# Sketched attention and a top-1 mixture of experts: one projection for keys and queries, the router inside kv, and a pipeline in written order

## The chip, the cores and the metric

One Trainium2 chip; the program runs on one of its cores. A core has five engines with queues of their own: PE (TensorE, matmuls into PSUM), DVE (VectorE), ACT (ScalarE), POOL (GpSimd, here also the indirect DMAs) and SP (the plain DMAs). The metric is the device time of one execution in microseconds, median of several runs; less is better. All data is float32.

## What is computed

```python
def phi(x):                      # 8 x 8 = 64 features of a token of one head (32 numbers)
    a = einsum('rd,bhsd->bhsr', S1, x); b = einsum('rd,bhsd->bhsr', S2, x)
    return outer product of a and b over r, flattened
# q, k, v: 4 batches, 4 heads, 1088 tokens, 32
kv = einsum('bhsf,bhsd->bhfd', phi(k), v);  z = phi(k) summed over tokens
x = (phi(q) @ kv) / (phi(q) @ z + 1e-6)          # then heads side by side: (4352, 128)
logits = x @ w_gate                              # 8 experts
e = argmax(logits); gate = softmax(logits)[e]
out[token] = gate * (relu(x @ w1[e]) @ w2[e])    # w1 128 x 1024, w2 1024 x 128
```

S1 and S2 arrive as float64. The kernel splits each into a float32 hi and lo half and multiplies with both.

## The kernel before

Batches are loaded as main tiles (1024 tokens, eight tiles of 128) and a remainder of 64 tokens, two batches' remainders to a tile. Names end in the batch and the chunk: a chunk is 4 tiles, 512 tokens, of all 4 heads.

*Keys*, per chunk: 4 transposes (L254), an eviction by ACT (L256), eight matmuls with hi and lo of S (L261, 64 columns), an eviction of the first half (L266), four outer products on DVE (L268), then eight matmuls that add [kv | z] of the batch in PSUM (L284). `kv_dup` and `kv_pair` are block-diagonal copies of it (L304, L305). *Queries*, per chunk: POOL lays q side by side with itself (L312), 8 transposes (L321), matmuls of 512 columns that make the features already transposed (L327), a product on DVE (L332), and [num | den] as matmuls with the features as left operand (L421), divided on DVE (L338 to L340). *Router*, per batch: x is transposed again (L354), multiplied with w_gate (L358), and DVE takes the argmax, the softmax weight and each token's rank among its expert's tokens (L368 to L405, with small bf16 matmuls L389 to L396). POOL then scatters each tile's rows to a table in DRAM by `row_i` (L407).

Behind the last scatter, tables of tiles are made on DVE (L468 to L508). *Experts*: 41 tiles of 128 rows. POOL gathers a tile's rows (L514), six tiles ahead; PE transposes (L522), multiplies with w1 (L538) and w2 (L551); ACT and DVE share the relu (L540, L541); POOL scatters to the output (L555).

In the attention part a scheduler sets each engine's order. In the experts, PE and DVE keep the written order. [...] PSUM tiles come from three pools: two wide ones (two banks each), three of a bank, and one for kv.

Of the kernel before, what the change touches and what calls it, by code (L numbers as in the profile page):

```python
# [38 lines left out]
def kernel(  # L39
# [78 lines left out]
    nc.sync.dma_start(out=s_words[0:R], in_=S1.bitcast(I32))  # L118
    nc.sync.dma_start(out=s_words[R:2 * R], in_=S2.bitcast(I32))
# [7 lines left out]
    load_main("q", q, 1)  # L127

# [4 lines left out]
    mask2 = const.tile([128, 2], FP, name="mask2")  # L133
    nc.gpsimd.memset(mask4, 0.0)
    nc.gpsimd.memset(mask2, 0.0)
    for g in range(4):
        nc.gpsimd.memset(mask4[g * D:(g + 1) * D, g:g + 1], 1.0)
        nc.gpsimd.memset(mask2[g * D:(g + 1) * D, g % 2:g % 2 + 1], 1.0)

    # Block-diagonal [kv | z]: of one head for two tiles (dup), of two heads for one tile (pair).  # L140
    kv_dup, kv_pair = [], []
    for b in range(B):
        kv_dup.append(big.tile([128, H, 2 * DA], FP, name=f"kv_dup{b}"))
        kv_pair.append(big.tile([128, NP, 2 * DA], FP, name=f"kv_pair{b}"))
        nc.gpsimd.memset(kv_dup[b], 0.0)
        nc.gpsimd.memset(kv_pair[b], 0.0)
# [4 lines left out]

    iota_p = const.tile([128, 1], FP, name="iota_p")
# [3 lines left out]
    upper = const.tile([128, 128], BF, name="upper")  # L156
    nc.vector.tensor_scalar(upper, col, iota_p, None, ALU.is_gt)
# [19 lines left out]

    # Tiles that the experts' rows are gathered into; rows past the end keep what was there.
# [9 lines left out]
    def bits(name, in_, s1, op0, s2=None, op1=None):  # L188
# [3 lines left out]
        else:  # L192
# [51 lines left out]
    v_rem_aug = big.tile([128, NR, H, DA], FP, name="v_rem_aug")
    nc.gpsimd.memset(v_rem_aug[:, :, :, D:DA], 1.0)
    nc.gpsimd.tensor_copy(out=v_rem_aug[:, :, :, 0:D], in_=v_rem)

# [1 line left out]
    def key_features(name, srcs, k_p, heads):  # L249
        """Features of the tokens of srcs (transposed source, four blocks of D each) into k_p."""  # L250
        n = len(srcs)
        kTp = bank_ps(f"kTp_{name}")
        for i, s in enumerate(srcs):
            nc.tensor.transpose(kTp[:, ts(i, 128)], in_=s, identity=ident)  # L254
        kT = att.tile([128, 512], FP, tag="kT", name=f"kT_{name}")
        nc.scalar.copy(out=kT[:, :n * 128], in_=kTp[:, :n * 128])  # L256
        ab = bank_ps(f"ab_{name}")
        for i in range(n):
            for t in range(2):
                # One start for the bank: it clears the flags of all of it.  # L260
                nc.tensor.matmul(ab[:, ts(i, 64)], lhsT=kT[:, ts(i, 128)],  # L261
                                 rhs=S12[t].rearrange("p h r -> p (h r)"), start=(i == 0 and t == 0),
                                 stop=(t == 1), skip_group_check=True)
        ab = ab[:, :n * 64].rearrange("p (g r) -> p g r", r=2 * R)
        a = att.tile([128, 4 * H, R], FP, tag="a", name=f"a_{name}")
        nc.scalar.copy(out=a[:, :n * 4], in_=ab[:, :, 0:R])  # L266
        for i in range(n):
            nc.vector.tensor_tensor(  # L268
                k_p[:, :, i] if heads else k_p[:, i],
                a[:, ts(i, 4), :, None].broadcast_to([128, 4, R, R]),  # L270
                ab[:, ts(i, 4), None, R:2 * R].broadcast_to([128, 4, R, R]), ALU.mult)

    k_p_rem = [big.tile([128, 1, H, R, R], FP, name=f"k_p_rem{r}") for r in range(NR)]

    def keys(b):
        k_sb, v_sb = main["k", b], main["v", b]
        v_aug = io.tile([128, H, J, DA], FP, tag="v_aug", name=f"v_aug{b}")
        nc.gpsimd.memset(v_aug[:, :, :, D:DA], 1.0)
        nc.gpsimd.tensor_copy(out=v_aug[:, :, :, 0:D], in_=v_sb)
# [7 lines left out]
        for c in range(NCH):  # L287
# [4 lines left out]
            for i in range(JC):  # L292
                add(flat[:, i, :], v_aug[:, :, c * JC + i, :], c == 0 and i == 0, False)
# [312 lines left out]
```

## Time and profile before

| | |
|---|---|
| median of 3 runs | 310.98 us (309.47 to 311.07) |
| span of the profiled execution, core 0 | 308.7 us (its own time is given by the span alone) |
| PE busy | 270.4 us (88%), mean granted clock 0.945 |
| VectorE / ScalarE / GpSimd busy | 118.6 / 80.0 / 137.2 us |
| HBM read / written | 17.81 / 4.95 MB |

Times are of one execution on the core. A busy PE is not a PE at its peak: an f32 matmul shows as two records, a transpose as one. The granted clock is in parts of 2.4 GHz, so 0.50 is 1.2 GHz.

### The profile page before, as it was taken

Reading aid. Unit: us, or ns where it says so; the run is one execution under the profiler, and the core shown is the slowest. Engines: PE = TensorE matmul, PEld = TensorE weight load, DVE = VectorE, ACT = ScalarE, POOL = GpSimd, SP = SyncE. Lnnn points to the kernel's source line nnn. Section 1 sums busy time; section 2 is a strip of 40 time slices with the busy share of each in tenths; the row PEclk is TensorE's granted clock in tenths of the full one; section 3 lists DMA queues with packets and bytes.
Section 4 is the critical chain, followed back from the end, with each engine's and each line's share of the span. In section 5 each row is a group of like instructions: output and inputs, shape, how many; then the busy total and the mean of one; then the engine's idle time right before and its main releaser. Section 6 shows DMA issues by size and latency. Waiting matters only on the chain.

```text
span 308.7 us, 6029 instructions
## 1 busy us (share of the span) xinstructions
PE 270.4 (88%) x2124; PEld 247.3 (80%) x2124; DVE 118.6 (38%) x383; ACT 80.0 (26%) x185; POOL 137.2 (44%) x177
## 2 busy tenths in 40 slices
PE   1899989999999996720399999999999999999994
PEld 1798867787787763620399999999999999999994
DVE  3513343645445552172133433333333333333320
ACT  1103124412412431100032233222233222332221
POOL 7430040380173074037665555555555555554313
PEclk9999999999999998555599999999999999999999
DMA  5799997010010011001111111111111111100000
GB/s 162 228 350 335 350 336 201 17 54 0 2 43 28 2 43 45 0 17 43 43 39 30 32 38 38 31 34 32 36 33 42 36 30 36 34 17 13 17 10 0
DMA packets 22988, 22.22 MB, mean 72 GB/s; under 512 B 5925, under 2 KB 20265, under 8 KB 22961
## 3 DMA queue, kind: packets, MB, share of 16 engines
q1 hardware_dynamic: 19248, 15.08, 16.3%
q0 software_dynamic: 3712, 6.77, 7.4%
q8 instruction: 18, 0.29, 0.4%
q14 instruction: 10, 0.07, 0.1%
HBM read 17.81 MB, written 4.95 MB: 74 GB/s over the span
## 4 chain that ended last, share of the span: by engine, by line
PE 46%; issue 3%; POOL 2%; DMA 1%; POOLq 0%; DVE 0%; ACT 0%; DVEq 0%
PE ph L538 23%; PE py L551 21%; PE xgTp L522 1%; POOL xs_dram L407 1%; POOL out_dram L555 1%; DMA xg<-xs_dram,grow 1%; POOLq L601 0%; DVE w L529 0%; ACT hT L540 0%; POOL xg L514 0%; DVE hT L541 0%; ACT xgT L524 0%; POOLq L555 0%; DVE to L531 0%; POOLq L514 0%
## 5 line engine op out<-in xcount | busy, mean ns | idle before, releaser
L538 PE MATMUL ph<-xgT,w 128*128 128x128 f32 x656 | 81.1, 278 | 0.0
L551 PE MATMUL py<-w_all,hT 128*128 x656 | 79.8, 275 | 0.0
L538 PEld LDWEIGHTS ph<-xgT,w 128*128 128x128 f32 x656 | 77.8, 195 | 0.0
L551 PEld LDWEIGHTS py<-w_all,hT 128*128 128x128 f32 x656 | 76.5, 192 | 0.0
L555 POOL DMA_INDIRECT out_dram<-y,to x41 | 41.7, 1018 | 61.8 <-ACT xgT L524 55.7
L541 DVE TENSOR_SCALAR hT<-ph 128x512 f32<-128x512 f32 x41 | 28.4, 692 | 94.4 <-ACT hT L540 94.4
L407 POOL DMA_INDIRECT xs_dram<-x,row_i x32 | 32.0, 999 | 49.9 <-DVE nt_i L472 15.1
L514 POOL DMA_INDIRECT xg<-xs_dram,grow x41 | 42.3, 1031 | 14.3 <-PE ph L538 10.1
L540 ACT ACTIVATE hT<-ph 128x512 f32<-128x512 f32 x41 | 24.5, 597 | 57.4 <-PE ph L538 56.3
L327 PE MATMUL qab<-qT,Srep 128*128 128x512 f32 x64 | 32.1, 608 | 1.4 <-ACT qT L323 1.4
L529 DVE COPY w<-w_all 128x1024 f32 x41 | 28.4, 692 | 1.3 <-DVE cj L501 0.8
L554 ACT ACTIVATE y<-py,xg 128x128 f32<-128x128 f32 x41 | 15.1, 368 | 49.0 <-PE py L551 49.0
L522 PE MATMUL xgTp<-ident,xg 128*128 128x128 f32 x41 | 11.5, 281 | 17.1 <-DMA xg<-xs_dram,grow 17.1
L421 PEld LDWEIGHTS nd<-kv_dup,q_pT 128*128 128x128 f32 x128 | 17.1, 208 | 6.8 <-DVE q_pT L332 5.5
L421 PE MATMUL nd<-kv_dup,q_pT 128*128 128x66 f32 x128 | 18.5, 295 | 4.0 <-DVE q_pT L332 3.5
L284 PEld LDWEIGHTS kv<-v_aug,k_p 128*128 128x128 f32 x128 | 17.9, 212 | 4.6 <-issue 3.7
L261 PE MATMUL ab<-S,kT 128*128 128x64 f32 x128 | 20.2, 313 | 1.4 <-ACT kT L256 1.3
L268 DVE TENSOR_TENSOR k_p<-a,ab 128x256 f32<-128x256 f32 x32 | 11.3, 417 | 25.4 <-ACT a L266 25.4
L261 PEld LDWEIGHTS ab<-S,kT 128*128 128x128 f32 x128 | 18.9, 228 | 2.7 <-ACT kT L256 2.7
L522 PEld LDWEIGHTS xgTp<-ident,xg 128*128 128x128 f32 x41 | 6.0, 145 | 17.4 <-issue 17.4
L284 PE MATMUL kv<-v_aug,k_p 128*128 128x66 f32 x128 | 18.6, 292 | 0.0
L330 ACT COPY qa<-qab 128x512 f32<-128x512 f32 x16 | 9.4, 586 | 27.7 <-PE qab L327 27.7
(164 smaller groups left out, 219.3 us busy)
## 6 DMA issues: line engine op xcount, KB each, us to landing
w_all<-in_moe_w_dram SPq DMA_DIRECT2D x16, 512.0 KB, 8.4
k<-in_k_dram SPq DMA_DIRECT2D x4, 512.0 KB, 5.9
v<-in_v_dram SPq DMA_DIRECT2D x4, 512.0 KB, 6.9
q<-in_q_dram SPq DMA_DIRECT2D x4, 512.0 KB, 8.4
xg<-xs_dram,grow POOLq DMA_INDIRECT x41, 2.5
out_dram<-y,to POOLq DMA_INDIRECT x41, 2.3
xs_dram<-x,row_i POOLq DMA_INDIRECT x32, 2.4
k_rem<-in_k_dram SPq DMA_DIRECT2D x4, 32.0 KB, 4.4
```

Of the source, the lines that this page charges most:

```text
L261: nc.tensor.matmul(ab[:, ts(i, 64)], lhsT=kT[:, ts(i, 128)], rhs=S12[t].rearrange("p h r -> p (h r)"), start=(i == 0 and t == 0), stop=(t ...
L284: nc.tensor.matmul(kv[:, ts(hp, 2 * DA)], lhsT=lhs[:, ts(hp, 128)], rhs=rhs[:, ts(hp, 2), :], start=(first and hp == 0), stop=last, skip_g ...
L327: nc.tensor.matmul(ab[:, t, :W], lhsT=Srep[t].rearrange("p g f -> p (g f)"), rhs=qT[:, g, :W], start=True, stop=True)
L407: d = nc.gpsimd.indirect_dma_start(out=xs_dram[:], out_offset=bass.IndirectOffsetOnAxis(ap=row_i[:, u:u + 1], axis=0), in_=x[:, u, :].bitc ...
L421: nc.tensor.matmul(o, lhsT=lhsT, rhs=kv_dup[b][:, h, :], start=True, stop=True)
L514: nc.gpsimd.indirect_dma_start(out=xg_bufs[j % XB].bitcast(I32), out_offset=None, in_=xs_dram[:], in_offset=bass.IndirectOffsetOnAxis(ap=g ...
L529: nc.vector.tensor_copy(out=w1, in_=w1_all[:, ds(wo, F)])
L538: nc.tensor.matmul(ph[:, ts(c, 128)], lhsT=w1[:, ts(c, 128)], rhs=xT, start=True, stop=True)
L540: nc.scalar.activation(hT[:, 0:512], ph[:, 0:512], AF.Relu)
L541: nc.vector.tensor_scalar(hT[:, 512:1024], ph[:, 512:1024], 0.0, None, ALU.max)
L551: nc.tensor.matmul(py[:, :DM], lhsT=hT[:, ts(c, 128)], rhs=w2_all[:, ds(wo + c * DM, DM)], start=(c == 0), stop=(c == NFC - 1))
L555: d = nc.gpsimd.indirect_dma_start(out=out[:], out_offset=bass.IndirectOffsetOnAxis(ap=st[j]["to"], axis=0), in_=y, in_offset=None, bounds ...
```

## The change

Keys and queries go through one function, `features`: four transposes, one matmul for each of the four 128-blocks with hi and lo of S side by side (128 columns), an eviction of the lo half, the sum of hi and lo, and one outer product of 1024 elements. Queries' features are then transposed (8 per chunk) and multiplied with `kvx`, which holds for each head [kv @ w_gate's rows of that head | kv | z]; the logits come out of the same matmul as num and den and are summed over heads. The old router's transposes and matmuls are gone. The remainders ride as a ninth tile of batches 1 and 3.

All engines keep the written order in the whole program. The order comes from a table of steps: `at(step, fn)` puts a piece into a step, and a step's pieces are written one after the other (transposes of a chunk in step s, its projection in s+1, accumulation of keys or transposes of features in s+3, num and den in s+4; the router in three further steps). Loads stand in another order, k, v and q have three buffers in place of two, and the words of S are loaded by ACT. The expert part keeps its code, and POOL and ACT keep the written order in it too.

```diff
+    ctx.enter_context(tc.manual_schedule())
-    io = ctx.enter_context(tc.tile_pool(name="io", bufs=2))
+    io = ctx.enter_context(tc.tile_pool(name="io", bufs=3))
...
     load_main("v", v, 0)
     load_rem(k_rem, k)
+    load_main("k", k, 1)
     load_rem(v_rem, v)
+    nc.sync.dma_start(out=w_gate, in_=moe_w_gate)
+    load_main("v", v, 1)
     load_main("q", q, 0)
-    nc.sync.dma_start(out=w_gate, in_=moe_w_gate)
-    load_main("k", k, 1)
-    load_main("v", v, 1)
     load_main("q", q, 1)
...
+        def project():
+            ab = bank_ps(f"ab_{name}")
+            for i in range(n):
+                nc.tensor.matmul(ab[:, ts(i, 128)], lhsT=st["xT"][:, ts(i, 128)],
+                                 rhs=s_cat.rearrange("p t g r -> p (t g r)"), start=True, stop=True)
...
+            nc.scalar.copy(out=lo, in_=ab[:, :, 1])
...
+            nc.vector.tensor_tensor(s4, ab[:, :, 0].rearrange("p i (g r) -> p i g r", g=4),
+                                    lo.rearrange("p i (g r) -> p i g r", g=4), ALU.add)
+            nc.vector.tensor_tensor(dst.rearrange("p g (a b) -> p g a b", a=R),
+                                    s[:, :, 0:R, None].broadcast_to([128, n * 4, R, R]),
+                                    s[:, :, None, R:2 * R].broadcast_to([128, n * 4, R, R]), ALU.mult)
+
+        at(step, turn)
+        at(step + 1, project)
...
+            p = bank_ps(f"kvg{b}")
+            nc.tensor.matmul(p[:, :H * E], lhsT=st["kvT"], rhs=gate_bd.rearrange("p h e -> p (h e)"),
+                             start=True, stop=True)
+            nc.vector.tensor_copy(out=kvx[b].rearrange("p n g c -> p (n g) c")[:, :, 0:E],
+                                  in_=p[:, :H * E].rearrange("p (h e) -> p h e", h=H))
...
+            tp = wide_ps(f"qp_{name}")
...
+                nc.tensor.transpose(tp[:, ts(i, 128)], in_=flat[:, ts(i, 128)], identity=ident)
+            t = att.tile([128, 1024], FP, tag="q_pT", name=f"q_pT_{name}")
+            w = n * NP * 64
+            nc.scalar.copy(out=t[:, 0:w], in_=tp[:, 0:w])
+            nc.vector.tensor_copy(out=t[:, w:2 * w], in_=tp[:, w:2 * w])
...
+                        nc.tensor.matmul(o, lhsT=lhsT, rhs=kvx[b][:, hp].rearrange("p g c -> p (g c)"),
+                                         start=True, stop=True)
...
+        at(step + 3, turn)
+        at(step + 4, num_den)
...
+        at(step, choose, 2)
+        at(step + 1, pick, 2)
+        at(step + 2, rank, 2)
...
+    key_chunk(0, 0, 0)
+    at(0, finish_s)
+    at(2, late_constants)
+    key_chunk(1, 0, 1)
...
+    query_rem(15, 1)
+    query_chunk(16, 3, 0)
+    query_chunk(17, 3, 1)
+    route(18, 2, J)
+    run(21)
+    route(22, 3, J + 1)
+    run(24)
...
-    with tc.manual_schedule(engines={PE, DVE}):
-        for j in range(AHEAD):
-            gather(j)
+    for j in range(AHEAD):
+        gather(j)
```

PE in a query chunk (batch 0, second chunk; a row with x8 stands for eight matmuls) before:

```order
L321 MATMUL qTp_0_1_473<-ident_114,q2_0_427 128x128 x8
L327 MATMUL qab_0_1_0_484<-qT_0_1_482,Srep0_244 128x512
L327 MATMUL qab_0_1_0_484<-qT_0_1_482,Srep1_248 128x512
L327 MATMUL qab_0_1_1_500<-qT_0_1_482,Srep0_244 128x512
L327 MATMUL qab_0_1_1_500<-qT_0_1_482,Srep1_248 128x512
L421 MATMUL nd_0_1_0_491<-kv_dup0_131,q_pT_0_1_0_489 128x66 x4
L321 MATMUL qTp_1_0_708<-ident_114,q2_1_705 128x128 x8
L421 MATMUL nd_0_1_1_507<-kv_dup0_131,q_pT_0_1_1_505 128x66 x4
L354 MATMUL xTp_0_0_517<-ident_114,x0_426 128x128 x4
```

and after (tp and ab: transposes and projection of a chunk, q or k; qp: its features transposed; nd_0_1: that chunk's logits, num and den):

```order
L286 MATMUL ab_q0_1_381<-s_cat_220,xT_q0_1_366 128x128 x4
L279 MATMUL tp_k1_1_391<-ident_126,k1_103 128x128 x4
L350 MATMUL kvg0_410<-gate_bd_224,kvT0_370 128x32
L373 MATMUL qp_0_0_413<-ident_126,q_p_0_0_231 128x128 x8
L286 MATMUL ab_k1_1_425<-s_cat_220,xT_k1_1_396 128x128 x4
L279 MATMUL tp_k2_0_435<-ident_126,k2_120 128x128 x4
L389 MATMUL nd_0_0_442<-kvx0_137,q_pT_0_0_422 128x82 x8
L373 MATMUL qp_0_1_459<-ident_126,q_p_0_1_232 128x128 x8
L286 MATMUL ab_k2_0_471<-s_cat_220,xT_k2_0_440 128x128 x4
L279 MATMUL tp_q1_0_481<-ident_126,q1_114 128x128 x4
L389 MATMUL nd_0_1_488<-kvx0_137,q_pT_0_1_468 128x82 x8
```

The 512-column matmuls are gone; transposes of features stand in their place, and pieces of three chunks alternate.

POOL at the start of the program (constants and the copies that put a column of ones beside v) before; the copies of v0 and v1 stand 18 and 22 rows behind iota_p:

```order
L149 IOTA iota_p_147 128x1
L149 IOTA col_149 128x128
L159 MEMSET ones_b_153 128x128
L149 IOTA rev_155 128x8
L149 IOTA ebase_157 128x8
L149 IOTA jio_161 128x41
L172 IOTA tokid_172 128x32
```

and after:

```order
L171 COPY v_aug0_151<-v0_97 128x32x32
L175 COPY v_rem_aug_149<-v_rem_88 128x8x32
L170 MEMSET v_aug1_155 128x32
L171 COPY v_aug1_155<-v1_110 128x32x32
L161 IOTA iota_p_158 128x1
L161 IOTA col_160 128x128
L183 MEMSET ones_b_162 128x128
L161 IOTA rev_164 128x8
L161 IOTA ebase_166 128x8
```

and VectorE after, where these constants are read between the features of the first and the second key chunk:

```order
L295 TENSOR_TENSOR k_p0_0_228<-sum_k0_0_254 128x1024
L252 TENSOR_SCALAR upper_221<-col_160,iota_p_158 128x128
L253 COPY base_e_222<-ebase_166 128x8
L255 TENSOR_SCALAR tri_223<-rev_164 128x8 x8
L256 TENSOR_TENSOR gate_bd_224<-w_gate_90,mask4_131 128x32
L293 TENSOR_TENSOR sum_k0_1_282<-ab_k0_1_275,lo_k0_1_280 128x4x4x16
L295 TENSOR_TENSOR k_p0_1_229<-sum_k0_1_282 128x1024
```

The iotas moved from ahead of both copies of v to behind them.

POOL at the end of the attention part (row scatters of a batch, then the first gather of the experts) before:

```order
L407 DMA xs_dram_255<-x1_704,row_i_1_857 34816x130 x8
L312 COPY q2_3_1233<-q3_884 128x16x64
L407 DMA xs_dram_255<-x2_964,row_i_2_1117 34816x130 x8
L407 DMA xs_dram_255<-x_rem_1144,row_i_rem_1223 34816x130 x2
L407 DMA xs_dram_255<-x3_1232,row_i_3_1385 34816x130 x8
L514 DMA xg0_177<-xs_dram_255,grow_1448 128x130
```

and after:

```order
L171 COPY v_aug3_630<-v3_400 128x32x32
L497 DMA xs_dram_227<-x0_454,row_i_0_701 34816x130 x8
L497 DMA xs_dram_227<-x1_652,row_i_1_944 34816x130 x9
L497 DMA xs_dram_227<-x2_897,row_i_2_1128 34816x130 x8
L497 DMA xs_dram_227<-x3_1057,row_i_3_1205 34816x130 x9
L608 DMA xg0_174<-xs_dram_227,grow_1271 128x130
```

The scatters of the remainders are now the ninth of batches 1 and 3, the latter in the last group.

## Rows read from the trace of the kernel before

**Rows 1.** The page: PE's busy tenths and clock in 40 slices; chain by line.
```profile
PE   1899989999999996720399999999999999999994
...
PEclk9999999999999998555599999999999999999999
...
PE ph L538 23%; PE py L551 21%; PE xgTp L522 1%; POOL xs_dram L407 1%; POOL out_dram L555 1%; DMA xg<-xs_dram,grow 1%; POOLq L601 0%; DVE w L529 0%; ACT hT L540 0%; POOL xg L514 0%; DVE hT L541 0%; ACT xgT L524 0%; POOLq L555 0%; DVE to L531 0%; POOLq L514 0%
```

**Rows 2.** Stretches: engines' busy time (instructions), granted clock, DMA share, GB/s.
```profile
7.40:24.80 17.40, 16.05 (x75) 15.22 (x75) 6.48 (x28) 2.68 (x7) 6.61 (x8) 1.00 0.94 290
24.80:120.80 96.00, 90.86 (x640) 70.21 (x638) 43.95 (x170) 28.38 (x52) 32.69 (x36) 1.00 0.36 111
120.80:152.40 31.60, 10.86 (x59) 9.46 (x60) 11.17 (x47) 1.69 (x4) 11.61 (x12) 0.50 0.07 23
152.40:308.70 156.30, 152.15 (x1352) 151.96 (x1351) 54.68 (x120) 45.92 (x122) 80.71 (x79) 0.99 0.11 29
```

**Rows 3.** The last chain in order of time: start, us, engine and line.
```profile
152.58 2.99 PE ph L538 x16
...
155.57 0.11 PE xgTp L522
155.68 1.79 PE ph L538 x16
157.47 1.79 PE py L551 x16
```

**Rows 4.** PE in order of time: start, us, what, idle before.
```profile
17.90 3.20 PE L284 MATMUL kv<-v_aug,k_p 128*128 128x66 f32 x14
...
21.31 0.42 PE L254 MATMUL kTp_rem<-ident,k_rem 128*128 128x128 f32 x1
...
24.30 1.06 PE L321 MATMUL qTp<-ident,q 128*128 128x128 f32 x4
...
25.37 1.73 PE L284 MATMUL kv<-v_aug,k_p 128*128 128x66 f32 x14
...
43.29 3.70 PE L327 MATMUL qab<-qT,Srep 128*128 128x512 f32 x8 [1.10 <-ACT qT L323]
...
120.86 1.98 PE L421 MATMUL nd<-kv_dup,q_pT 128*128 128x66 f32 x8 [2.15 <-DVE q_pT L332]
```

**Rows 5.** Groups, 0 to 155 us: busy us, mean ns | idle before.
```profile
L268 DVE TENSOR_TENSOR k_p<-a,ab 128x256 f32<-128x256 f32 x32 | 11.3, 417 | 25.4 <-ACT a L266 25.4
L332 DVE TENSOR_TENSOR q_pT<-qa,qab 128x512 f32<-128x512 f32 x16 | 10.9, 683 | 6.7 <-ACT qa L330 6.5
...
L330 ACT COPY qa<-qab 128x512 f32<-128x512 f32 x16 | 9.4, 586 | 27.7 <-PE qab L327 27.7
...
L340 DVE TENSOR_TENSOR x<-nd,den 128x256 f32<-128x256 f32 x16 | 6.4, 420 | 4.5 <-DMA xs_dram<-x,row_i 4.2
...
L339 DVE RECIPROCAL den<-den 128x8 f32<-128x8 f32 x16 | 3.0, 204 | 0.2
```

**Rows 6.** All engines in order of time, the stretch of the tail.
```profile
123.69 1.97 PE L421 MATMUL nd<-kv_dup,q_pT 128*128 128x66 f32 x8 [0.85 <-DVE q_pT L332]
...
132.60 0.23 DVE L368 TENSOR_REDUCE top<-lg 128x8 f32<-128x64 f32 x1 [6.04 <-PE lg L358]
132.86 0.22 DVE L370 TENSOR_TENSOR sh<-lg,top 128x64 f32<-128x64 f32 x1
...
135.16 0.17 DVE L404 CAST row_i<-row 128x8 int32<-128x8 f32 x1
...
135.61 0.98 POOL L407 DMA_INDIRECT xs_dram<-x,row_i  x1 [15.13 <-DVE nt_i L472]
...
148.19 1.04 POOL L514 DMA_INDIRECT xg<-xs_dram,grow  x1 [2.14 <-issue]
```

**Rows 7.** All engines in order of time, the start: v of batch 1.
```profile
9.84 0.51 SPq L103 DMA_DIRECT2D v<-in_v_dram  x1
...
16.81 1.04 POOL L279 COPY v_aug<-v 128x1024 f32<-128x1024 f32 x1 [2.89 <-DMA v<-in_v_dram]
```

More of the change, by code (lines that the diff above doesn't have):

```diff
@@ L244 @@
[L244 to L249, printed above, removed]
-        n = len(srcs)
[L252 to L271, printed above, removed]
@@ new lines, in late_constants @@
+    def late_constants():
+        nc.vector.tensor_scalar(upper, col, iota_p, None, ALU.is_gt)
+        nc.vector.tensor_copy(out=base_e, in_=ebase)
+        for e in range(E):
+            nc.vector.tensor_scalar(tri[:, e, :], rev, float(E - e) - 0.5, None, ALU.is_ge)
+        nc.vector.tensor_tensor(gate_bd, w_gate[:, None, :].broadcast_to([128, H, E]),
+                                mask4[:, :, None].broadcast_to([128, H, E]), ALU.mult)
+    upper = const.tile([128, 128], BF, name="upper")
@@ new lines, with kv_add, key_chunk, accumulate @@
+    k_p_rem = [big.tile([128, H, RR], FP, name=f"k_p_rem{r}") for r in range(NR)]
+    kv = {}
+    def kv_add(b, lhs, rhs, first, last):
+        for hp in range(NP):
+            nc.tensor.matmul(kv[b][:, ts(hp, 2 * DA)], lhsT=lhs[:, ts(hp, 128)], rhs=rhs[:, ts(hp, 2), :],
+                             start=(first and hp == 0), stop=last, skip_group_check=True)
+    def key_chunk(step, b, c):
+        k_sb = main["k", b]
+        k_p = att.tile([128, JC * H, RR], FP, tag="k_p", name=f"k_p{b}_{c}", bufs=3)
+        features(f"k{b}_{c}", step,
+                 [k_sb[:, h, ts(c, JC), :].rearrange("p j d -> p (j d)") for h in range(H)], k_p)
+        def accumulate():
+            if c == 0:
+                kv[b] = ps_kv.tile([128, 512], FP, tag="kv", name=f"kv{b}")
+            flat = k_p.rearrange("p g f -> p (g f)")
+            for i in range(JC):
+                kv_add(b, flat[:, ts(i, H * RR)], v_aug[b][:, :, c * JC + i, :], c == 0 and i == 0, False)
+        at(step + 3, accumulate)
@@ new lines, in x_tile, with rows_of, query_chunk @@
+    def x_tile(b):
+        if b not in x_of:
+            x_of[b] = (rt.tile([128, J + 1, XW], FP, tag="x", name=f"x{b}", bufs=3),
+                       rt.tile([128, J + 1, H * E], FP, tag="lgh", name=f"lgh{b}"))
+        return x_of[b]
+    def rows_of(b, j, n):
+        x, lgh = x_tile(b)
+        return x[:, ds(j, n), 0:DM], lgh[:, ds(j, n)]
+    def query_chunk(step, b, c):
+        query(f"{b}_{c}", step,
+              [main["q", b][:, h, ts(c, JC), :].rearrange("p j d -> p (j d)") for h in range(H)],
+              b, lambda: rows_of(b, c * JC, JC), None)
@@ new lines, in rank @@
+        def rank():
+            x, oh = st["x"], st["oh"]
+            pr = bank_ps(f"pr_{b}")
+            nc.tensor.matmul(pr[:, 0:n * E], lhsT=upper, rhs=oh[:, :n * E], start=True, stop=False,
+                             skip_group_check=True)
+            for u in range(1, n + 1):
+                nc.tensor.matmul(pr[:, u * E:(n + 1) * E], lhsT=ones_b, rhs=oh[:, 0:(n + 1 - u) * E],
+                                 start=False, stop=(u == n), skip_group_check=True)
+            rk = t3("rk")
+            nc.vector.tensor_tensor(rk, pr[:, 0:n * E].rearrange("p (u e) -> p u e", e=E),
+                                    base_e.unsqueeze(1).to_broadcast([128, n, E]), ALU.add)
+            nc.vector.tensor_tensor(rk, rk, oh[:, :n * E].rearrange("p (u e) -> p u e", e=E), ALU.mult)
+            row = t2("row")
+            nc.vector.tensor_reduce(row, rk, AX.X, ALU.add)
+            row_i = t2("row_i", I32)
+            nc.vector.tensor_copy(out=row_i, in_=row)
+            nc.vector.tensor_tensor(base_e, base_e, pr[:, ts(n, E)], ALU.add)
+            for u in range(n):
+                d = nc.gpsimd.indirect_dma_start(
+                    out=xs_dram[:], out_offset=bass.IndirectOffsetOnAxis(ap=row_i[:, u:u + 1], axis=0),
+                    in_=x[:, u, :].bitcast(I32), in_offset=None, bounds_check=E * NTOK - 1, oob_is_err=False)
+                tc.declare_no_dep(d.ins, group="scatter", reason="every token has a row of its own")
+                tc.add_to_no_dep_group("scatter", d.ins)
@@ new lines, in route, with more, load, run @@
+        at(step, choose, 2)
+        at(step + 1, pick, 2)
+        at(step + 2, rank, 2)
+    def more(names, b):
+        def load():
+            for name, src in names:
+                load_main(name, src, b)
+        return load
+    def run(last):
+        for i in sorted(steps):
+            if i <= last:
+                for _, _, fn in sorted(steps.pop(i), key=lambda f: f[:2]):
+                    fn()
+    key_chunk(0, 0, 0)
+    at(0, finish_s)
+    at(2, late_constants)
+    key_chunk(1, 0, 1)
@@ new lines @@
+    key_rem(2, 0)
+    key_end(4, 0)
+    key_chunk(2, 1, 0)
+    query_chunk(3, 0, 0)
+    query_chunk(4, 0, 1)
+    key_chunk(5, 1, 1)
+    key_end(8, 1)
+    at(2, lambda: load_experts(range(0, E // 2)))
+    at(5, more([("k", k), ("v", v)], 3))
+    run(5)
+    augment(2)
+    key_chunk(6, 2, 0)
+    query_chunk(7, 1, 0)
+    query_chunk(8, 1, 1)
+    query_rem(9, 0)
+    key_rem(9, 1)
+    key_chunk(10, 2, 1)
+    key_end(13, 2)
+    route(9, 0, J)
+    at(8, lambda: load_main("q", q, 3))
```

396 lines of the change are left out of this document (176 added, 220 removed).

## The prediction, made before the changed kernel was run

> **What bounds the kernel now.** I read the page's slices first, then the chain, the stretches, and single rows of PE's order of time. PE is busy nine tenths of nearly every slice, and the granted clock falls to half only around the middle [rows 1]. The chain that ended last is almost all L538 and L551, the experts [rows 1]. Cut at 152.4 us, the stretches say why: from there to the end PE is busy 152.15 of 156.3 us [rows 2]. One tile there takes 1.79 + 1.79 us of matmuls and a transpose of 0.11 [rows 3], so 41 tiles are 151 us in a row without a gap, and no line of that stage changes its work. What the change can move is the 152.4 us ahead of it: a start at the lower clock to 24.8, a dense stretch to 120.8 (PE 90.86 of 96.0), and a tail of 31.6 us in which PE works 10.9 [rows 2]. The 156.3 us behind are a floor.
>
> The clock needs a second look. The stretch from 7.4 to 24.8 is given as 1.00 [rows 2], but there 14 records of L284 take 3.20 us, and from 25.37 on 14 of the same take 1.73 [rows 4]: the first ran at 1.2 GHz, the second at 2.4. PE had been busy at the lower level since 14.4, with the narrow products (64 and 66 columns); the pitch halved behind 13 transposes that stand between 21.31 and 25.4 (first and last of four groups in [rows 4]). It fell again at 120.8, after PE had waited 2.15 us for a DVE product [rows 4].
>
> **PE's work.** A record of at most 128 columns costs 1.79/16 = 0.112 us at 2.4 GHz [rows 3]; one of 512 costs 3.70/8, or 0.45 without the last one's way out [rows 4]. An f32 matmul is two records, a transpose one. A key chunk had 4 transposes, 16 records of L261 and 16 of L284: 36, or 4.0 us; it keeps 4 + 8 + 16 = 28, or 3.1. A query chunk had 8 + 4 transposes, 16 of L421, 8 of L358 (36 narrow, 4.0 us) and 8 wide ones of L327 (3.6): 7.6 us; it gets 4 + 8 transposes, 8 records of projection and 16 of [logits | num | den]: 36, or 4.0. Eight of each: 93 us become 57. With the remainders, kv gate and rank products some 64 us remain after.
>
> **VectorE's work** rises against it. Priced by [rows 5]: the sum of hi and lo (256 elements) 0.42 as k_p. The outer product of 1024 has no row; 256 cost 0.417 and 512 cost 0.683, so 1.22 on that line. Its bounds are 0.68 (a 512 row) and 1.67 (four of 256). I take 1.22, since both rows are of the same operation; a chunk's features are then 1.64. Half of the transposed features out of PSUM: 0.65 (a 512 row), behind ScalarE's half of 0.59, since both write one tile. Den and reciprocal (0.20 each at most), the logits (128 elements, between 0.20 and 0.42, say 0.28) and two products of 0.42: 1.4 with their overlap. Routing's small steps, 0.26 from one to the one that needs it (132.60 and 132.86 in [rows 6]), are 0.95 for the choice, 1.7 for the pick with its copy of token ids, 1.05 for the rank. ScalarE has five evictions in a full step, of 0.59 at most, 3 us: it binds nowhere.
>
> **The steps.** With these prices PE's work in steps 4 to 20 is 3.6, 3.3, 2.5, 4.1, 5.4, 3.0, 2.0, 4.4, 3.4, 3.9, 3.3, 2.1, 3.7, 5.4, 1.2, 1.4, 3.0: 55.6 us. VectorE's is 2.1, 1.6, 2.5, 3.8, 3.6, 2.6, 3.7, 4.8, 3.4, 3.0, 2.6, 4.2, 3.8, 3.6, 2.8, 3.4, 3.2: 54.6. Two queues of equal length, each in its written order, must wait for each other. Following them row by row, PE stands for VectorE in steps 7 and 8 (0.4 together), 10 to 13 (3.4, behind the pick and the rank), 16 and 17 (3.2, the same), and 19 and 20 (4.9: nd_r1 needs kvx3's gate columns, whose copy stands behind the choice of batch 2). That is 12 us. Batch 2's row_i then comes 2.0 us behind the last PE work of step 20, since the rank stands behind a normalization and an eviction. So 55.6 + 12 + 2.0 = 69.6 us from the start of step 4. After the long wait in step 19 I take the clock as fallen, as at 120.8: one transposed chunk and one num/den at half speed, +2.7.
>
> **The start of step 4.** Step 0 can start when k0 is in, about as now. But POOL now copies both v tiles before it writes iota_p and col, and VectorE's constants from these stand ahead of the second chunk's features. v1 was issued at 9.84 and its copy began at 16.81, waiting on it [rows 7]; now one load fewer stands ahead, so between 12 and 16.8: 14.5. Copy 1.04, iotas and constants 1.8, features 1.64: the accumulation of step 4 could start at 19. PE's own work before it (three chunks, one accumulation) gives 19.4 if the clock rises early and 21.7 if it doesn't. I take 20, bounds 17 and 24.
>
> **The tail.** At present the last num/den starts at 123.69, logits end at 132.60, and row_i is cast at 135.16 [rows 6]; 8 scatters at (148.19 - 135.61 - 2.4)/8 = 1.27 us follow (2.4 is the landing of the last one), then the gather, 4.2 us to the first expert product. Removed: two groups of transposes, evictions and logits. But POOL now has batch 2's 8 scatters and batch 3's 9 back to back: 17 x 1.27 = 21.6 us outlast batch 3's own num/den and routing (3.7 + 5 us, within the first 8), so they are the path: 0.3 + 21.6 + 2.4 + 4.2 = 28.5. The shorter route is hidden there. That cover goes only if batch 3's row_i comes over 10 us after batch 2's.
>
> **Sum.** 20 + 69.6 + 2.7 + 28.5 = 120.8 us to the first expert product, against 152.4: 31.6 us less. Span 308.7 - 31.6 = 277.1. No time of the profiled execution but its span is given; the runs' median is 2.3 above that, which I add: 279.4, so 280. Loads don't bind: they now end near 50 us, and the second half of k, v, q is wanted after 45. The larger buffers add no work, and hand order on POOL and ScalarE in the experts leaves PE's 3.68 us a tile, since gathers run six tiles ahead.
>
> **Rivals.** *The clock stays low in part of the stage* (300). [...] For it: the narrow products from 14.4 to 21 didn't raise it, and a wait of 2.15 us ended it. Against: transposes and 128-column products are now over half of the records, and the first expert tile, 16 records in 2.99 us, was enough to get the next at 1.79 [rows 3]. Half of 55.6 us at half speed costs 28 less some 6 of waits that vanish: 302. The Trainium skill, page TensorE: Matmul & The Clock Gate, Part 4 (PE-mode transpose), states that transposes don't bring the full clock. By that rule the stage would stay low for longer; the trace differs, with the pitch halving right behind 13 transposes.
> *It stays low all through, and the kernel is slower.* Some 558 records at 3.20/14 = 0.229 us are 128 us; 5 for the load and 2 for the first wait, then 5 of routing, 11.4 for nine scatters, 6.6 to the first product: 158 against 152.4, so 317. It needs over six sevenths of the stage at 1.2 GHz; before, that held for 17 us only.
> *Faster than forecast.* The clock is up by 12 us, v1 lands early, and the outer product is nearer 0.9 us: 3 at the start, 4 of PE's waits, 3 of clock: 269.
> *The gain is hidden.* The route from the last row to the first gather stays, and if loads or POOL rather than PE paced the stage nothing would move. POOL's 34 scatters are 43 us in four parts with pauses, and loads end at 50: I see no place for it.
>
> **How the numbers follow.** Forecast 0.55 (270 to 290: the bounds of the start, -3 and +4, of the outer product, 13 in these steps of which half of +-0.5 us lies on the path, +-4, and the clock's 2.7); clock low in part 0.27 (290 to 309); slower 0.06; faster than forecast 0.10; hidden 0.02. 267 to 300 leaves out some 0.18. A measurement of this kernel can tell about 0.5% from no change: faster 0.92, same 0.02, slower 0.06.
>
> **What would show it.** Right: the first expert product near 121 us; PE busy near 60 us ahead of it at 2.4 GHz; 17 scatters in a row at its end; features of 1024 at 1.2 us; a wait of 3 us at nd_r1. Wrong: a record pitch of 0.2 us between 25 and 85; VectorE free while PE waits on loads; scatters with a pause between batch 2 and 3.

## The result, and the profile after

The changed kernel takes **277.4 us** (median of 5 runs, 276.34 to 280.64) against 311.07 us of the kernel before beside it (5 runs): ratio **.891 [.886, .895]**. The profiled execution, with a span of 278.9 us, was the slowest of the five; ratios leave out executions that the clock disturbed, medians and ranges take all.

The page: PE's busy tenths and the clock in 40 slices, and the chain by line; they answer to [rows 1].

```profile
PE   1799998896959400069999999999999999999994
...
PEclk9999999999685755559999999999999999999999
...
PE ph L632 26%; PE py L645 24%; PE kv L308 7%; PE nd L389 5%; POOL xs_dram L497 4%; PE ab_q L286 3%; PE ab_k L286 3%; PE qp L373 2%; PE xgTp L616 2%; PE tp_k L279 1%; DVE q_p L295 1%; PE tp_q L279 1%; DMA s_words<-in_S_dram 1%; POOL out_dram L649 1%; DMA xg<-xs_dram,grow 1%
```

The experts' two lines have half of the chain, as before, and the dip in PE's row now comes at a third of the span. Stretches, cut at step 4's first product, shortly behind batch 3's first accumulation (which starts at 58.05), at the end of batch 2's ranks and at the first expert product (columns as in [rows 2]):

```profile
0.00:19.25 19.25, 11.54 (x62) 10.67 (x63) 8.21 (x35) 4.41 (x9) 7.60 (x40) 1.00 0.89 259
19.25:60.76 41.51, 39.40 (x355) 38.24 (x354) 30.46 (x76) 14.43 (x39) 9.09 (x10) 1.00 0.78 253
60.76:91.49 30.73, 24.61 (x175) 23.16 (x173) 19.80 (x62) 6.68 (x19) 11.94 (x11) 0.78 0.08 27
91.49:121.75 30.26, 3.27 (x30) 2.79 (x29) 14.04 (x53) 0.89 (x3) 20.05 (x20) 0.56 0.13 42
121.75:278.90 157.15, 152.96 (x1352) 152.77 (x1351) 54.88 (x119) 45.91 (x122) 80.39 (x79) 0.99 0.10 29
```

The experts take 157.15 us where they took 156.3 [rows 2]: their work is the same, and the whole gain lies ahead of 121.75. The attention part has two halves. To 60.76 PE is busy 39.40 of 41.51 us. From there it is busy 24.61 of 30.73, at a mean clock of .78. PE in order of time shows why (columns as in [rows 4]):

```profile
12.18 2.08 PE L286 MATMUL ab_k<-s_cat,xT_k 128*128 128x128 f32 x8 [0.68 <-ACT xT_k L281]
...
15.12 2.69 PE L308 MATMUL kv<-v_aug,k_p 128*128 128x66 f32 x16
...
19.25 1.90 PE L308 MATMUL kv<-v_aug,k_p 128*128 128x66 f32 x16
...
64.42 1.99 PE L389 MATMUL nd<-kvx,q_pT 128*128 128x82 f32 x16 [1.04 <-DVE kvx L352]
...
69.27 1.98 PE L389 MATMUL nd<-kvx,q_pT 128*128 128x82 f32 x16 [1.07 <-DVE x L407]
71.09 3.32 PE L308 MATMUL kv<-v_aug,k_p 128*128 128x66 f32 x16
...
83.57 0.50 PE L394 MATMUL nd_r<-kvx,q_pT_r 128*64 128x82 f32 x6 [2.94 <-DVE kvx L352]
84.00 1.09 PE L373 MATMUL qp<-ident,q_p 128*128 128x128 f32 x8
85.77 3.70 PE L389 MATMUL nd<-kvx,q_pT 128*128 128x82 f32 x16 [0.67 <-ACT q_pT L376]
89.26 1.91 PE L373 MATMUL qp<-ident,q_p 128*128 128x128 f32 x8
...
91.91 2.01 PE L389 MATMUL nd<-kvx,q_pT 128*128 128x82 f32 x16 [0.41 <-ACT q_pT L376]
```

Eight records of ab_k take 2.08 us at 1.2 GHz (12.18); sixteen of kv take 1.90 us at 2.4 GHz (19.25) and 3.32 where the level is low (71.09). The group at 15.12 changes over within itself. Behind waits of 1.04 (at 64.42) and 1.07 us the pitch (the time from one record to the next) doubles at 71; behind the wait of 2.94 us it doubles again at 85.8.

All engines in the tail, which answers to [rows 6]:

```profile
93.26 0.17 DVE L494 CAST row_i<-row 128x8 int32<-128x8 f32 x1
...
93.70 0.97 POOL L497 DMA_INDIRECT xs_dram<-x,row_i  x1 [10.48 <-DVE base_e L495]
...
98.90 0.17 DVE L494 CAST row_i<-row 128x9 int32<-128x9 f32 x1 [0.17 <-DVE row L492]
...
114.38 0.97 POOL L497 DMA_INDIRECT xs_dram<-x,row_i  x1 [0.30 <-issue]
...
117.58 1.04 POOL L608 DMA_INDIRECT xg<-xs_dram,grow  x1 [2.23 <-DMA xs_dram<-x,row_i]
...
121.75 3.64 PE L632 MATMUL ph<-xgT,w 128*128 128x128 f32 x16
```

Batch 3's row_i is there at 98.90 while POOL still scatters batch 2; 17 scatters run without a pause to 115.4, and PE has nothing to do for 22 us.

### The profile page after: what moved, and what is told of

The parts are those of the page before. It is cut to its first block, busy times and chain, and to the rows that moved or that the text cites. A ratio compares the mean times of both kernels' runs of the same rounds, so it can differ in the third digit from the quotient of the medians.

```text
span 278.9 us, 5661 instructions
## 1 busy us (share of the span) xinstructions
PE 231.8 (83%) x1965; PEld 227.6 (82%) x1965; DVE 127.4 (46%) x345; ACT 72.3 (26%) x190; POOL 129.1 (46%) x160
## 4 chain that ended last, share of the span: by engine, by line
PE 74%; DVE 7%; issue 7%; POOL 6%; DMA 3%; ACT 2%; POOLq 1%; ACTq 0%; DVEq 0%
PE ph L632 26%; PE py L645 24%; PE kv L308 7%; PE nd L389 5%; POOL xs_dram L497 4%; PE ab_q L286 3%; PE ab_k L286 3%; PE qp L373 2%; PE xgTp L616 2%; PE tp_k L279 1%; DVE q_p L295 1%; PE tp_q L279 1%; DMA s_words<-in_S_dram 1%; POOL out_dram L649 1%; DMA xg<-xs_dram,grow 1%
## 5 line engine op out<-in xcount | busy, mean ns | idle before, releaser
L497 POOL DMA_INDIRECT xs_dram<-x,row_i x34 | 35.6, 1047 | 42.3 <-DVE den L401 22.3
L389 PE MATMUL nd<-kvx,q_pT 128*128 128x82 f32 x128 | 17.4, 294 | 3.2 <-ACT q_pT L376 1.1
L389 PEld LDWEIGHTS nd<-kvx,q_pT 128*128 128x128 f32 x128 | 16.5, 209 | 3.8 <-ACT q_pT L376 1.4
L308 PE MATMUL kv<-v_aug,k_p 128*128 128x66 f32 x128 | 17.5, 296 | 0.0
L618 ACT COPY xgT<-xgTp 128x128 f32<-128x128 f32 x41 | 10.6, 258 | 24.9 <-PE xgTp L616 24.9
L625 DVE TENSOR_TENSOR to<-xg,inv_i 128x1 int32<-128x1 int32 x41 | 6.3, 154 | 16.6 <-DMA xg<-xs_dram,grow 12.6
L286 PE MATMUL ab_k<-s_cat,xT_k 128*128 128x128 f32 x64 | 10.5, 316 | 1.1 <-ACT xT_k L281 0.7
L279 PE MATMUL tp_k<-ident,k 128*128 128x128 f32 x32 | 6.3, 331 | 5.6 <-DMA k<-in_k_dram 4.7
L286 PEld LDWEIGHTS ab_k<-s_cat,xT_k 128*128 128x128 f32 x64 | 9.4, 226 | 1.6 <-ACT xT_k L281 1.1
```

The source lines that it names most:

```text
L286: nc.tensor.matmul(ab[:, ts(i, 128)], lhsT=st["xT"][:, ts(i, 128)], rhs=s_cat.rearrange("p t g r -> p (t g r)"), start=True, stop=True)
L308: nc.tensor.matmul(kv[b][:, ts(hp, 2 * DA)], lhsT=lhs[:, ts(hp, 128)], rhs=rhs[:, ts(hp, 2), :], start=(first and hp == 0), stop=last, ski ...
L389: nc.tensor.matmul(o, lhsT=lhsT, rhs=kvx[b][:, hp].rearrange("p g c -> p (g c)"), start=True, stop=True)
L497: d = nc.gpsimd.indirect_dma_start(out=xs_dram[:], out_offset=bass.IndirectOffsetOnAxis(ap=row_i[:, u:u + 1], axis=0), in_=x[:, u, :].bitc ...
```

## The experiments

Twelve kernels in four groups, each group on one chip. The kernel before took 320.6 us on the chip of group e, 311.1 on that of a, 315.8 on that of b and 321.5 on that of c, so kernels are compared within a group, by the difference of their ratios times the time of the kernel before; only group a holds a repeat of the changed kernel. On the three chips that were slower PE, ScalarE and VectorE also stand still for up to 5.4 us at a time with nothing shown that they wait for (last section).

**e1: the scheduler in place of the written order.** The new work, with the attention part ordered by the scheduler as before.

```diff
-    ctx.enter_context(tc.manual_schedule())
...
+    with tc.manual_schedule(engines={PE, DVE}):
```

> The new work in the scheduler's order: the attention part is no longer in written order, the experts keep PE and VectorE in written order as before the change. Theory (the gain is PE's removed work, 93 us down to 57 for the chunks): most of it stays, 277 to 288 us. Rival (the gain is the written order): 298 to 310 us.

277.76 us (274.54 to 282.69), .858 [.856, .860]. The gain is there without the written order, so it comes with the new work (its loads and buffers went with it and were not tried apart).

**e2: PE's projection twice.** Each projection matmul is issued twice; the result stays.

```diff
-            for i in range(n):
+            for i in [i for i in range(n) for _ in range(2)]:
```

> Each projection matmul is issued twice into the same place: 136 more records of 128 columns, 15.2 us of PE at 2.4 GHz. Theory (PE paces most steps, with some 9 us of waits in the stage): 286 to 291 us, 9 to 14 more, since only waits can take the rest. Rival (VectorE paces): 277 to 281. If the clock stays up all through because of the added dense products, up to 5 us less than the theory's numbers.

301.26 us (299.78 to 302.18), .940 [.936, .945]: 26.4 more than e1, above both. **e3: VectorE's outer product twice.**

```diff
+            for _ in range(2):
                 nc.vector.tensor_tensor(dst.rearrange("p g (a b) -> p g a b", a=R),
```

> Each outer product is issued twice into the same place: 16 of 1.22 us and 4 of 0.42 us more on VectorE, 21 us. Theory (both queues are equally long, so either one's growth shows): VectorE becomes the longer one by 15 us in steps 4 to 20, 288 to 296 us. Rival (PE alone paces, VectorE's work is cover): 277 to 283 us.

298.7 us (297.11 to 301.89), .931 [.926, .937]: 23.4 more than e1, above both too; some 21 of VectorE work had been added. PE in e2, then in e3 (step 4, batch 3's first chunk, the remainder's num/den):

```profile
20.76 1.90 PE L308 MATMUL kv<-v_aug,k_p 128*128 128x66 f32 x16
...
66.81 1.96 PE L308 MATMUL kv<-v_aug,k_p 128*128 128x66 f32 x16
...
101.35 0.81 PE L394 MATMUL nd_r<-kvx,q_pT_r 128*64 128x82 f32 x6 [5.92 <-DVE kvx L352]
```

```profile
19.56 2.00 PE L309 MATMUL kv<-v_aug,k_p 128*128 128x66 f32 x16
...
65.73 1.90 PE L309 MATMUL kv<-v_aug,k_p 128*128 128x66 f32 x16
...
98.53 0.81 PE L395 MATMUL nd_r<-kvx,q_pT_r 128*64 128x82 f32 x6 [7.48 <-DVE kvx L353]
```

From step 4 to batch 3's first accumulation the changed kernel needs 38.8 us (19.25 to 58.05). e2 needs 46.1: of 76 more records, 8.5 us, 7.3 show. e3 needs 46.2: of 11.8 us more of outer products 7.4 show. In neither stretch does an engine stand still over 0.3 us with nothing shown. In this first half PE binds: it is busy 36.69 of the changed kernel's 38.8 us. VectorE has 10.0 us to spare there, of which 4.4 took up the added work. In the second half both kernels wait longest where the changed one did, at nd_r. There the totals can't be read as prices, since both lost clock (the last two num/den took 3.7 us each), both had unexplained pauses, and e1 has another order.

**e4: batch 2's routing a step earlier.**

```diff
-    route(18, 2, J)
+    route(17, 2, J)
```

> The router of batch 2 starts one step earlier (17 for 18), so its 8 scatters start some 5 us earlier, while nd_r1 waits about 1 us longer. Theory (17 scatters in a row are the path to the experts): 273 to 275 us, 2 to 4 less, until batch 3's own rows are the last. Rival (batch 3's num, den and routing are the path already): 277 to 279 us.

283.16 us (279.36 to 285.48), .876 [.870, .882]: 5.7 more than e1, a miss for both. PE's wait, then VectorE's casts and POOL:

```profile
90.19 0.81 PE L394 MATMUL nd_r<-kvx,q_pT_r 128*64 128x82 f32 x6 [4.12 <-DVE kvx L352]
```

```profile
94.92 0.17 DVE L494 CAST row_i<-row 128x8 int32<-128x8 f32 x1
...
108.34 0.17 DVE L494 CAST row_i<-row 128x9 int32<-128x9 f32 x1 [0.17 <-DVE row L492]
...
108.79 0.97 POOL L497 DMA_INDIRECT xs_dram<-x,row_i  x1 [3.52 <-DVE cnt L563]
```

Now the pick stands ahead of the copy of the gate columns too, and nd_r waits 4.12 us. The casts are 13.4 us apart, more than the 10.2 of eight scatters, and POOL stands idle for 3.52 us between the two batches: batch 3's own row_i ends the part, and the earlier routing of batch 2 buys nothing. The 5.7 us are not its price alone, since PE also stood still for 2.18 us up to 84.4 with nothing shown that it waited for, and e1 has another order.

**a1: the repeat.**

> The changed kernel once more, with nothing edited, as the measure for the three others on the same chip. On the chip of the first four experiments the kernel before took 3% longer than where the change was timed, so this one is expected at .88 to .90 of the kernel before by every theory; if the ratio differs, the change is worth something else on another chip.

279.01 us (276.37 to 281.49, 8 runs), .891 [.888, .894]; the same ratio as the result.

**a2: the gate columns' copy on ScalarE.**

```diff
-            nc.vector.tensor_copy(out=kvx[b].rearrange("p n g c -> p (n g) c")[:, :, 0:E],
+            nc.scalar.copy(out=kvx[b].rearrange("p n g c -> p (n g) c")[:, :, 0:E],
```

> The copy of the eight gate columns per head out of PSUM (kvx <- kvg) goes from VectorE to ScalarE; nothing else moves. Theory (PE stands for VectorE's written order, not for its sum of work): this copy ended PE's waits of 0.92, 1.04 and 2.94 us in the profile of the change, and ScalarE is idle then, so the three waits together fall from 4.9 to under 1.5, batch 2's row_i is cast some 3 us earlier, the scatters with it, and the time falls by 3 to 5 us against the repeat (the clock may stay up too). Rival (VectorE's work is as long as PE's, so it only moves the wait): the 0.18 us copy is all that VectorE loses, PE waits a step later, and the time is within 1 us of the repeat.

275.45 us (272.68 to 279.81), .879 [.875, .883]: 1.4% under the repeat, and the intervals don't meet. PE, then the cast:

```profile
12.21 1.16 PE L286 MATMUL ab_k<-s_cat,xT_k 128*128 128x128 f32 x8 [0.68 <-ACT xT_k L281]
...
17.09 1.90 PE L308 MATMUL kv<-v_aug,k_p 128*128 128x66 f32 x16
...
75.28 0.50 PE L394 MATMUL nd_r<-kvx,q_pT_r 128*64 128x82 f32 x6 [0.18 <-ACT kvx L352]
...
79.02 2.85 PE L389 MATMUL nd<-kvx,q_pT 128*128 128x82 f32 x16 [2.21 <-DVE x L407]
```

```profile
85.60 0.17 DVE L494 CAST row_i<-row 128x8 int32<-128x8 f32 x1
```

From step 4 to row_i it is 68.5 us, where the repeat needs 74.0. The wait at nd_r is gone, but the rival has a share: 2.21 us appear two groups later, behind VectorE's normalization of that same nd_r. All waits together fall only from 8.6 to 7.1 us. The rest of the 5.5 us is clock: in this execution the kv group that took 3.30 in the repeat (at 71 us) took 1.94. This profile also started early, at 17.09, which the edit does not touch; so the ratios say what the edit is worth, some 3.9 us.

**a3: PE's waits filled from step 13 on.** `fill` issues identity by identity into unused columns of kv's bank.

```diff
+            nc.tensor.matmul(kv_bank[:, 256:384], lhsT=ident, rhs=ident, start=False, stop=False, skip_group_check=True)
...
+    at(13, lambda: fill(3), 0)
...
+    for step, n in ((16, 4), (17, 4), (20, 2), (21, 1)):
+        at(step, lambda n=n: fill(n), 0)
+    at(19, lambda: fill(12), 0.5)
```

> Products that nothing reads (128 x 128, identity by identity, 0.22 us each at the upper level) stand in six of PE's waits from step 13 on: 3, 4, 4, 12, 2 and 1 of them. Theory (the falls of the clock behind these waits cost time on the path): kv in step 16 at 1.9 instead of 3.3 us, nd in step 20 at 2.0 instead of 3.7, 5.8 us of PE's time less, of which 3 to 6 us show against the repeat. Rival (the clock's falls are hidden by VectorE, or the added products push work back): between 1 us less and 2 us more.

275.44 us (274.10 to 277.56), .887 [.883, .890]. PE:

```profile
79.02 2.92 PE L269 MATMUL kv_bank<-ident 128*128 128x128 f32 x24
...
82.41 0.50 PE L400 MATMUL nd_r<-kvx,q_pT_r 128*64 128x82 f32 x6 [0.18 <-DVE kvx L358]
...
84.61 2.01 PE L395 MATMUL nd<-kvx,q_pT 128*128 128x82 f32 x16 [0.23 <-ACT q_pT L382]
```

The stretch from step 4 (21.28) to row_i (89.57) is 68.3 us, 5.7 less than the repeat, where 5.8 of lost clock were counted: PE's longest wait was nearly as long, and the clock held. That is what a clock at its upper level is worth there, in these two executions. The ratios differ by 1.4 us only, and their intervals meet, so in time the gain is not certain.

**a4: the start and the tail filled too.**

```diff
+    nc.vector.memset(kv_bank[:, 256:384], 0.0)
...
+    at(0, lambda: fill(6), 0)
     key_chunk(0, 0, 0)
+    at(0, lambda: fill(4))
...
+    at(23, lambda: fill(12), 3)
     run(24)
+    fill(84)
```

> As the run with the middle filled, and besides: 6 and 4 such products at the start (ahead of and behind the first transposes), 12 ahead of the last rank and 84 behind it, while POOL scatters. Theory (each stretch at the lower level costs what the pitch doubles): the first expert tile at 1.8 instead of 3.6 us, so 1.8 less; at the start the first three chunks' products at the upper level, up to 2.5 less; with the middle 6 to 10 us less than the repeat. Rival: the start waits for transfers and VectorE, the tail for POOL, so only the first expert tile shows: 2 us less, or 2 more if the products themselves are late.

276.89 us (276.18 to 277.85), .892 [.889, .895]: as the repeat, a miss. PE:

```profile
8.25 2.90 PE L271 MATMUL kv_bank<-ident 128*128 128x128 f32 x12 [8.25 <-DVE kv_bank L267]
10.94 1.06 PE L287 MATMUL tp_k<-ident,k 128*128 128x128 f32 x4
...
93.89 19.00 PE L271 MATMUL kv_bank<-ident 128*128 128x128 f32 x168
116.38 0.47 PE L632 MATMUL xgTp<-ident,xg 128*128 128x128 f32 x1 [3.49 <-DMA xg<-xs_dram,grow]
...
117.95 3.73 PE L648 MATMUL ph<-xgT,w 128*128 128x128 f32 x16
```

At the start the products waited for the clearing of their tile, which stood on VectorE behind the preparation of S, so k0's transposes came at 10.94 instead of 4.68. In the tail they ended 3.49 us too soon, and the first expert tile ran at the lower level all the same. One thing it did: the spread of the runs is 1.7 us, where the repeat's is 5.1.

**b1: a2, and the start filled rightly.** Clearing first on VectorE; 7 products ahead of k0, 4 behind its transposes.

> The gate columns' copy on ScalarE, and products that nothing reads (identity by identity) at the start alone: 7 while PE waits for k0 until 4.7 us, 4 in the wait of 1.95 us behind the first transposes; the tile that they write is cleared as VectorE's first instruction, so they delay nothing (in the run that filled all waits this clearing stood behind the preparation of S, and the first transposes came at 10.9 instead of 4.7 us). Theory (the clock rises at 12 us in one execution and at 21 in another, since PE's work up to there is broken by waits, and this is most of the spread between executions): step 4's accumulation starts by 17.1 in the profile, the median falls 2 to 3 us below that of the run with the copy on ScalarE alone (275.45 on its chip, .885 of the kernel before by medians), and the executions lie within 3 us of each other instead of 7. Rival (the spread has another source, such as transfers): same median within 1 us and the same spread.

282.44 us (277.95 to 284.61), .889 [.881, .896]; the spread stayed. **b2: a2, and batch 2's routing early** (the edit of e4).

> The gate columns' copy on ScalarE, and the choice, pick and rank of batch 2 one step earlier. Moved alone, that routing put the pick ahead of the gate copy in VectorE's queue and the kernel got slower. Theory (the loss was that copy's place, and the scatters of batch 2 are the path): with the copy off VectorE's queue nd_r waits under 0.5 us, batch 2's row_i is cast about 3 us earlier, and the time is 2 to 4 us below that of the run with the copy on ScalarE alone, until batch 3's row_i, 4.6 us of slack later, binds. Rival (the pick delays the queries' features of batch 3 instead, so its row_i moves later and takes over): between 1 us less and 3 more.

280.69 us (279.15 to 281.85), .889 [.885, .893]. **b3: the changed kernel with POOL's constants ahead of its copies of v** (the two `augment` calls and v_rem's copy stand behind the iotas).

> The changed kernel with POOL's iotas and constants written ahead of its copies of v, as before the change; no other edit. The prediction's term for the start of step 4 had VectorE's constants wait behind these copies. Theory from the profile of the change (VectorE waits 1.24 us for col at 14.0, but PE is busy until the accumulation of step 4, which waits for nothing): the wait goes, and the time stays within 1 us of the changed kernel (277 to 279, .891 of the kernel before). Rival (the term is real, since the features of the second chunk are late by it): 1.2 us less.

287.61 us (284.15 to 288.06), .907 [.901, .913]. By the ratios, as far as those of two chips can be compared, b1 and b2 lie 3.2 and 3.3 us over a2, and b3 lies 5.1 over the changed kernel: no theory came true in time. But none of the three totals settles its question. In all three ScalarE's copy of a lo half came 2.6 us behind its product and held PE for 2.0 to 2.1 us (at 63.3 us in b1; nothing of it at that place in the repeat), and b2's nd_r waited 3.31 us for nothing shown. What their traces show all the same: in b1 the clock is up by the first projection, PE then waits 0.98 and 0.60 us for VectorE, and VectorE for POOL (VectorE, then PE):

```profile
14.81 0.29 DVE L259 TENSOR_SCALAR upper<-col,iota_p 128x128 bf16<-128x128 f32 x1 [2.97 <-POOL col L168]
```

```profile
17.67 2.00 PE L315 MATMUL kv_bank<-v_aug,k_p 128*128 128x66 f32 x16 [0.60 <-DVE k_p L302]
```

In b2 the casts are 13.6 us apart (89.29, 102.89), as in e4: the cover of batch 3's routing is gone. In b3 VectorE has no wait for col, and PE, with the clock low to 20.7, begins step 4 at 21.36.

**c1: together.** a2 with b3's order on POOL, b1's start, and fills of 5, 8, 1, 12, 90 and 3 in the later waits.

> What the runs so far point to, in one kernel: the gate columns' copy on ScalarE; products that nothing reads in PE's waits (7 and 4 at the start, 5, 8 and 1 ahead of steps 17, 20 and 21, 12 ahead of the last rank, 90 while POOL scatters, 3 between the first two transposes of the experts); POOL's iotas and constants ahead of its copies of v. Theory: with the clock up early, VectorE waited 2.97 us for col at 14.8 and PE 0.98 and 0.60 for VectorE, so with both edits the accumulation of step 4 starts at 16 (17.67 with the clock alone, 19.25 in the changed kernel); nd of batch 3 at 2.0 instead of 2.9 to 3.7 us; the first expert tile at 1.8 to 2.2 instead of 3.6. From the 275.45 us of the copy on ScalarE alone (.885 of the kernel before by medians): 3 less at the start, 1 in the middle, 1.6 at the experts, so about .867 of the kernel before. Rival (only the copy is worth anything; fills push work back where ScalarE or VectorE come late): .88 to .89.

295.19 us (293.58 to 300.14), .918 [.914, .922]: above both, and above the changed kernel's ratio. PE:

```profile
15.77 1.90 PE L314 MATMUL kv_bank<-v_aug,k_p 128*128 128x66 f32 x16
...
88.78 1.91 PE L395 MATMUL nd<-kvx,q_pT 128*128 128x82 f32 x16
...
116.28 0.37 PE L150 MATMUL kv_bank<-ident 128*128 128x128 f32 x1 [1.05 <-issue]
...
138.06 0.27 PE L628 MATMUL xgTp<-ident,xg 128*128 128x128 f32 x1
...
138.94 1.95 PE L644 MATMUL ph<-xgT,w 128*128 128x128 f32 x16
```

Each part did at its place what the theory said: step 4 at 15.77, nd of batch 3 at 1.91 us, the first expert tile at 1.95. But the 90 products of the tail, 19.0 us for 84 in a4, took 40 here. From 102 to 118 us PE issued one record in about 1.4 us, and the first expert transpose came at 138.06. The first gather had been issued at 118.44, and such a row lands 2.6 us behind (the page's median): some 17 us lost to products that nothing needed.

So a2 is the version that beats both kernels on one chip.

## Why the prediction was right

By its own steps, predicted and measured in the profiled execution:

| step | predicted us | measured us |
|---|---|---|
| start of step 4 | 20 | 19.25 |
| PE's work, steps 4 to 20 | 55.6 | 58.1 |
| PE's waits in them | 12 | 8.2 |
| clock | 2.7 | 5.9 |
| to batch 2's row_i | 2.0 | 1.8 |
| tail | 28.5 | 28.5 |
| first expert product | 120.8 | 121.75 |
| span | 277.1 | 278.9 |

Measured work is 72.24 us from 19.25 to 91.49, less waits and clock; the clock's 5.9 is the sum of what each slow group took over its like at the upper level (3.32 - 1.94, 1.12 - 0.66, 2.08 - 1.16, 1.06 - 0.60, 3.70 - 2.01, 1.91 - 1.07, and 0.2 of small ones).

**PE's work** carries the result, and was 2.5 us more than its sum: e1 has the gain without the order. **The outer product** of 1024 takes 1.22 us, as taken:

```profile
23.77 1.22 DVE L295 TENSOR_TENSOR q_p<-sum_q 128x1024 f32<-128x1024 f32 x1
```

**The waits** were put right at the end (3 us at nd_r1 behind kvx3's copy; 2.94 measured, and a2 takes it away), and too high in between: up to 60.76 VectorE has 11 us to spare, and PE waits 2.1 us in all there. The two queues were not of equal length: in steps 4 to 20 VectorE is busy 50.3 us, 4.3 under its sum. Its load binds where routing and normalization meet the remainders. **The clock** was mis-sized: the term had one fall in it, the trace has two, and the one at 71 us follows waits of only 1.0 and 1.1 us. What decides such a fall is not shown: in a2 waits of 0.60 and 1.43 us at the same place left the pitch as it was (kv 1.94). Waits and clock err by 3.8 too much and 3.2 too little, which nearly cancels; that the sum came so near is in part luck. That the clock stays low in part, the rival at 302, was thus right in kind for 12 of 72 us, not for half.

**The start** came near its number, but VectorE's path was priced too long: POOL copied v1 from 12.38 on, not from 14.5, and the second chunk's features, behind a wait of 1.24 us for col, were ready at 16.8, not at 19. PE, at the lower level to about 17, was the later one. Its two cases were put at 19.4 and 21.7; a2, at the upper level from 12.2, starts step 4 at 17.09, and b3, low to 20.7, at 21.36. b1 shows a third case: with the clock up, the constants bind, at 17.67; with them moved ahead in c1, step 4 begins at 15.77.

Of the clock, the Trainium skill (page TensorE: Matmul & The Clock Gate, Part 4, PE-mode transpose) states that transposes don't bring the full level. In the changed kernel transposes are 5 of the 29 records between 12.18 and 17.6, and the level rose all the same; no run here has transposes alone.

**The tail** was right to 0.1 us: 17 scatters at 1.29 ((114.38 - 93.70)/16) are the path, 28.5 us from row_i to the first product, and 28.5, 28.8 and 28.5 in a2, a3 and a4, wherever row_i stood. Its condition held too: where batch 2's routing came early (e4, b2), the casts were over 13 us apart, and batch 3's own became the end.

**The time.** The profiled execution's span is 1.8 over the sum: 0.95 at the first expert product, 0.85 in the experts, whose first tile took 3.64 us. Its own time, 280.64, is 1.7 over its span, where 2.3 was taken. The other four runs were 3.1 to 4.3 us shorter than it, so the median lies 2.6 under the forecast.

## What to carry to other kernels

When a change removes work from a bound engine, price the work first and the waits of the new order last, and look stage by stage at which engine has time to spare; equal sums over a whole part say little. A small copy that another engine waits for should not stand behind long work in a queue when a third engine is idle: 0.18 us of copy, moved, were worth 1.4%. Filling a wait held the clock where the wait was known (a3), though its gain in time is not certain; it cost some 17 us where the filler itself came late (c1), so it belongs only where no transfer's landing is in question.

## What the hardware showed beside that

**When the clock rises at the start differs between executions.** Step 4 began at 17.09 (a2), 19.25 (after), 19.27 (a1), 21.28 (a3) and 21.36 (b3) us with nothing edited ahead of it in the first four: the projection at 12.2 took 1.16 us in a2 and 2.08 in the others. The repeat's runs spread by 5.1 us, and those of a4, at the upper level from its first projection on, by 1.7; but those of b1, at that level as early, spread by 6.7, on a chip with pauses. What makes the spread is not shown, since one execution of each kernel was profiled.

**Chips differ in pauses.** In steps 4 to 20 (20 to 92 us) the five profiles on chips where the kernel before takes 311 us show no pause of PE's products, VectorE or ScalarE over 0.3 us in which an instruction waits for nothing shown. On the other three chips each profile has some, the longest between 0.9 us (e3) and 5.4 (b2). ScalarE, PE and VectorE of b2 (total, times, longest):

```profile
ACT kvn L338 <- issue: 5.7, 2, 5.4
...
PE nd_r L394 <- issue: 3.3, 1, 3.3
DVE sum_q L293 <- issue: 3.0, 2, 2.4
```

The Trainium skill (page Runtime: NRT & Kernel Launch, Instruction fetch mechanics) states that engines stream their instructions in blocks through a DMA queue, mostly hidden. The page of the profile has such a queue (q8, 19 packets, 0.31 MB in c1; 17 and 0.28 MB in the changed kernel, which has no such pauses), and late instructions are one possible reason; no run here shows that they were the cause. It stays open, and with it what b1, b2, b3 and c1 would take on a chip without pauses.
